# Two layers of attention and feed-forward on one core: the input of layer one's projections moves from the tile xf into four rows of the gelu tile g, and the order is picked anew

## The chip, the cores and the metric

The kernel runs on one core of a Trainium2 chip. The time is that of one execution on the device, in microseconds (us). Before the change it is 1430.3 us, the median of three runs (1429.61 to 1430.81).

TensorE (PE) multiplies matrices and writes to PSUM, ScalarE (ACT) computes exponentials and gelus, VectorE (DVE) does copies, additions and layernorms, GpSimd (POOL) works on integers in SBUF, and SyncE (SP) issues the DMAs. PEld is the weight loading of TensorE.

## The reference

One sequence of 2048 tokens, width 512, in bf16, goes twice through the same two blocks, with the same weights. The attention has 32 heads of 16.

```python
def _A_ref(x, wqkv, wo):
    qkv = (x @ wqkv).reshape(B, S, 3, H, Dh) ...
    scores = jnp.einsum("bhqd,bhkd->bhqk", q, k) * (Dh ** -0.5)
    p = _softmax(scores, axis=-1)
    o = jnp.einsum("bhqk,bhkd->bhqd", p, v)
    return (o back to B, S, D) @ wo
def _B_ref(x, w1, b1, w2, b2):            # F = 1792
    h = _gelu(jnp.einsum("bsd,df->bsf", x, w1) + b1)
    return jnp.einsum("bsf,fd->bsd", h, w2) + b2
x = A_x
x = x + _A_ref(_layernorm(x), A_wqkv, A_wo)
x = x + _B_ref(_layernorm(x), B_w1, B_b1, B_w2, B_b2)
x = x + _A_ref(_layernorm(x), A_wqkv, A_wo)
x = x + _B_ref(_layernorm(x), B_w1, B_b1, B_w2, B_b2)
```

## The kernel before

**Cells.** The 2048 queries are cut into four segments of 512 (the last one of layer one into two of 256). A score cell is one matmul (L1432): 128 keys by 512 columns of queries, for one group of heads. There are 4096 cells in both layers. ScalarE computes the exponential of most cells, two or three at a time, from PSUM into units of 512 columns called "pt" (`exps`, L1879). VectorE takes other cells: it writes one scaled integer form of the scores (L1601, into the tiles "du"), POOL makes three more from it by integer additions (L1691, L1695), and the four are multiplied with scaled copies of V. The product with V (`pvs`, L1945) takes one matmul for a cell of ScalarE and four for one of VectorE. Four such matmuls stand side by side in TensorE.

**Units.** There are 20 pt units of their own. More are lent by tiles that are idle for a while: Q once a segment's attention is done, parts of K and V, and the 14 rows of the gelu tile `G` (128 x 14 x 512). `lent_g` gives the rows of `G` to the exponentials when a segment's feed-forward is done ("gfree"), and takes all of them back once the next segment's layernorm has landed, before its feed-forward may begin ("g1"). A search takes the first free units in a fixed sequence of blocks: first the own ones, then the lent ones.

**Around the attention.** While the attention of a segment runs, the post-processing of the segment before runs beside it (`post`): the output projection (`wo`, added to x at L1046), a layernorm (`ln`; its last step on VectorE is L802, the normalisation is L828) which a DMA transpose (L834) writes into the tile `XF`, seven pairs of up-projections (`hpair`, matmuls of L647, bias added by VectorE into `G` at L1155), the gelu in two halves (L1176), and four down-projections (`ytile`, added to x at L1207). In layer zero a second layernorm follows, with the same transposes, and twelve projections of layer one for that segment's 512 tokens (`projections`, `proj`): four K, four V, four Q, copied out of PSUM at L912 and L930. All of these matmuls are issued through L647.

**What xf holds.** In layer zero `XF` holds first the input of the feed-forward and then, after the second layernorm, the input of the projections of layer one. So in `post` the next segment's layernorm has two gates: "xfree" (all pairs of the previous feed-forward have read `XF`) and, when the previous segment was in layer zero, "pfree" (all twelve projections have read it):

```python
gate = [("xfree",) + prev] if prev else []
if prev and prev[0] == 0:
    gate.append(("pfree",) + prev)
```

**Order.** The order of each engine's instructions is fixed when the kernel is built. Each piece of work is a thread with a rank (a low number goes first): 10 for `wo`, 12 for the pairs and the gelu, 13 for the down-projections, 15 for the projections of layer one. `when` lets parts begin after a set share of the following attention has been scored. A model of the engines' clocks (`_Sched.run`) takes at each step the instruction that could start first. Twelve constants of that model (`KNOBS`) are set anew after each 24 us (`STRETCH`) of ScalarE's time, from one of 16 rows (`ORDERS`), chosen by the 60 entries of `PICKS`. A gate is therefore a matter of this order: an instruction whose token comes later is placed later in its engine's queue, and the engine does other work in the meantime. In the chip's program semaphores protect each tile.

**Queues.** SP issues weight loads and transposes in one queue. The weights go through a ring of five buffers of 256 KB ("wr", L1098), and a load waits until its buffer is free.

Of the kernel before, what the change touches and what calls it, by code (L numbers as in the profile page):

```python
# [18 lines left out]
NDC = D // 128  # L19
# [5 lines left out]
THIRD = (2, 5)  # L25
PT_RING = 20
WSEG = 2
LEND = (1, 0)
QP_RING = 3
W_RING = 5  # L30
# [80 lines left out]
)  # L111
STRETCH = 24
PICKS = (1, 13, 1, 1, 13, 13, 1, 2, 1, 13, 1, 13, 13, 1, 1, 14, 1, 13, 13, 13, 13, 11, 3, 1,
         1, 13, 13, 13, 13, 13, 13, 1, 13, 13, 13, 1, 13, 1, 1, 1, 1, 3, 13, 13, 5, 1, 13, 13,
         1, 0, 1, 1, 13, 13, 13, 13, 1, 1, 1, 13)
LOG2E = 1.4426950408889634
E_SCALE = 0.25 * LOG2E * 128
E_BIAS = 15992.765054484162
# [145 lines left out]
class _Sched:  # L264
# [164 lines left out]
    def tune(self):  # L429
        k = min(int(self.clock["act"] // STRETCH), len(PICKS) - 1)  # L430
        if k != self.stretch:
            self.stretch = k
            globals().update(zip(KNOBS, ORDERS[PICKS[k]]))
            LATENCY["pe"] = PE
# [84 lines left out]
def bass_interleave_layers__mha_block__dense_activation_gelu__prompt_kernel(  # L519
# [15 lines left out]
    with ExitStack() as es:  # L535
# [18 lines left out]
        T["WR"] += [pt[:, PT_RING - 4 + 2 * i:PT_RING - 2 + 2 * i, :].rearrange("p c f -> p (c f)") for i in range(2)]  # L554
        T["PT"] = [pt[:, :, :]] + [T["K"][1][:, :, 512 * c:512 * c + 512] for c in LEND]
        T["PT"] += [T["Q"][:, :, 512 * c:512 * c + 512] for c in range(S // 512)]
# [80 lines left out]
class _Plan:  # L637
# [221 lines left out]
    def proj(self, l, kind, i, c, src, skeys, ph, done):  # L859
# [53 lines left out]
        if kind == "K":  # L913
            keys = ["K%d.%d.%d" % (l, i, c)]
            if l == 1:
                keys += ["XL.%d" % t for t in range(4 * c, 4 * c + 4)]
                if c in LEND:
                    yield ("need", ("k1", c))
                    keys += self.lentkeys(LEND.index(c))
                elif c >= 2:  # L920
# [3 lines left out]
        elif kind == "Q":  # L924
            if l:
                yield ("need", ("q1", 0, c))
            yield _Op(ev, DV, lambda e: copy(e, T["Q"][:, i, cols], pb), reads=["B.%d" % b] + first,
                      writes=["Q.%d.%d" % (i, c)] + (self.lentkeys(len(LEND) + c) if l else []))
        else:
# [7 lines left out]
    def projections(self, l, c, prio):  # L937
        T = self.T
        if l == 0:
            def src(dc, t):  # L940
                return T["K"][1][:, dc, t * 128:(t + 1) * 128] if t is not None else T["K"][1][:, dc, 512 * c:512 * c + 512]
            skeys = ["XL.%d" % t for t in range(4 * c, 4 * c + 4)]
        else:
            def src(dc, t):
                return T["XF"][:, dc, (t % 4) * 128:(t % 4) * 128 + 128] if t is not None else T["XF"][:, dc, :]
            skeys = ["XF.%d" % j for j in range(4)]
        ph = self.phase[c]
        units = []
        if l == 1:
            units = [("K", b) for b in range(4)] + [("V", 4 * c + b) for b in range(4)] + [("Q", b) for b in range(4)]  # L950
        else:
            for b in range(4):
                units.append(("K", b))
                if c == 0:
                    units.append(("Q", b))
                units.append(("V", 4 * c + b))
            if c > 0:
                units += [("Q", b) for b in range(4)]
        for j, (kind, i) in enumerate(units):
            p = prio + (0.01 * j if l else 0.5 if kind == "Q" and c > 0 else 0)  # L960
            if l:
                yield ("cond", self.when(0, (c, 0, 512), JB + JS * j))
            if l == 0 and kind == "Q" and c > 0:
                yield ("cond", lambda i=i: self.scored >= QAT[c] + QSTEP * i)
            yield ("spawn", self.proj(l, kind, i, c, src, skeys, ph, (kind, l, i, c)), p)
# [136 lines left out]
    def wmore(self):  # L1102
        self.wover = {}
        yield ("cond", lambda: self.scored >= self.base[(NL - 1, self.segs[-1][WSEG])])
        us = range(PT_RING - 4, PT_RING)
# [74 lines left out]
    def ytile(self, l, seg, t):  # L1180
# [30 lines left out]
        if l == NL - 1:  # L1211
            yield _Op("sp", 1.0, lambda e: e.dma_start(self.hbm["out"][:, t, :], T["X"][:, t % XT, :]), reads=["X.%d" % (t % XT)],
                      writes=["OUT.%d" % t], sem="dout", by=16, tail=2.0)
            yield ("give", ("xout", t))

    def when(self, l, seg, part):
        return lambda: self.scored >= min(self.base[(l, seg)] + part * self.span[(l, seg)], self.total)

# [5 lines left out]
    def post(self, l, seg):  # L1224

        T = self.T
        tiles = self.tiles(seg)
        c = seg[0]
        last = (l, seg) == (NL - 1, self.segs[l][-1])
        prev = self.before(l, seg)  # L1230
        hb, hs, yb, ys = PACE.get((l, c), (HB[l], HS[l], YB[l], YS[l]))
        yield ("need", ("otn", l, seg, 3))
        for t in tiles:
            yield ("spawn", self.wo(l, seg, t), 10)
        self.phase[c] = 2 * l + 1
        xf, xk = lambda t: T["XF"][:, :, (t % 4) * 128:(t % 4) * 128 + 128], lambda t: ["XF.%d" % (t % 4)]
        gate = [("xfree",) + prev] if prev else []
        if prev and prev[0] == 0:
            gate.append(("pfree",) + prev)
        for ts in ([t] for t in tiles) if last else (tiles,):  # L1240
            yield ("spawn", self.ln(ts, xf, xk, LNP, last, gate), 0.2 if last else LNP)
        for t in tiles:
            yield ("need", ("xready", t, 2 * l + 1))
        yield ("give", ("ofree", l, seg))
        for t in tiles:
            yield ("need", ("lnt", t, 2 * l + 1))
        yield ("need", ("g1", l, seg))
        for p in range(NFC // 2):
            yield ("cond", self.when(l, seg, hb + hs * p))
            yield ("spawn", self.hpair(l, seg, p), 12 + 0.1 * p)  # L1250
        if not last:
            yield ("spawn", self.gelu(l, seg), 12)
        if not last:
            for p in range(NFC // 2):
                yield ("need", ("h", l, seg, p))
            yield ("give", ("xfree", l, seg))
        for i, t in enumerate(tiles):
            yield ("cond", self.when(l, seg, yb + ys * i))
            yield ("spawn", self.ytile(l, seg, t), 13)
        if l < NL - 1:  # L1260
            self.phase[c] = 2 * l + 2
            xp, pk = lambda t: T["XF"][:, :, (t % 4) * 128:(t % 4) * 128 + 128], lambda t: ["XF.%d" % (t % 4)]
            for ts in (tiles[:2], tiles[2:]):
                yield ("spawn", self.ln(ts, xp, pk, LNP), LNP)
        for t in tiles:
            yield ("need", ("xready", t, 2 * l + 2))
        yield ("give", ("gfree", l, seg))
        if l == NL - 1:
            return
        for t in tiles:  # L1270
            yield ("need", ("lnt", t, 2 * l + 2))
        yield from self.projections(l + 1, c, 15)
        for kind in "KVQ":
            for i in range(4):
                yield ("need", (kind, l + 1, 4 * c + i if kind == "V" else i, c))
        yield ("give", ("pfree", l, seg))
# [457 lines left out]
    def setup_units(self):  # L1734
        self.blocks, self.alias, self.closed = [(0, PT_RING)], {}, set()
        for c in LEND:
            lo = self.blocks[-1][1]
# [28 lines left out]
    def lent_g(self):  # L1766
        lo, hi = self.blocks[self.gblock]
        for c in range(self.NQ):
            for kind in "KVQ":
                for i in range(4):  # L1770
                    yield ("need", (kind, 0, 4 * c + i if kind == "V" else i, c))
        for l in range(NL):
            for seg in self.segs[l]:
                prev = self.before(l, seg)
                if prev:
                    yield ("need", ("gfree",) + prev)
                if seg[1] == 0:
                    self.closed.difference_update(range(lo, hi))
                    for u in range(lo, hi):
                        yield ("rel", "pt", u)  # L1780
                    for t in self.tiles(seg):
                        yield ("need", (GBACK[0], t, 2 * l + GBACK[1]))
                    self.closed.update(range(lo, hi))
                    for u in range(lo, hi):
                        yield ("take", ("pt", u))
                yield ("give", ("g1", l, seg))

# [6 lines left out]
    def lend_units(self):  # L1794
        for i, c in enumerate(LEND):
            self.s.spawn(self.lent(c, *self.blocks[1 + i]), 4)
# [261 lines left out]
```

## Time and profile before

| | us |
|---|---|
| median of three runs | 1430.3 |
| the profiled execution | 1429.75 |
| its span, first to last instruction | 1427.9 |
| ScalarE busy | 1401.1 |
| TensorE matmuls busy | 1385.5 |
| VectorE busy | 1216.6 |
| POOL busy | 997.9 |
| last L1018 of layer zero's segments, start | 196.2, 371.7, 542.9, 716.2 |
| last L1018 of layer one's first segment, start | 951.6 |

L1018 is the transpose of a finished piece of attention output. Four of them end a segment's attention, so these marks cut the span into stages: between two marks runs the attention of one segment with the post-processing of the one before. The last mark ends a longer stage, because layer one's first two segments begin on the keys that are ready and finish later.

A line of the groups in the profile reads: line, engine, operation, tile written <- tiles read, shape, count | busy us, mean ns of one | idle us of the engine before them, and what ended it. The granted clock of TensorE was 1.000 over the whole span.

### The profile page before, as it was taken

What the parts mean: (1) busy time and instruction counts of PE and PEld (TensorE: products, weight loads), DVE (VectorE), ACT (ScalarE), POOL (GpSimd) and SP (SyncE); (2) the same over time, 40 slices, a digit from 0 to 9 for tenths busy, and PEclk for the clock granted to TensorE, in tenths of its full rate; (3) what the DMA queues carried; (4) which work ended last, traced back from release to release, by engine and by line L of the source; (5) the groups of instructions that cost most, each with busy time, mean ns of one, the idle gap of its engine ahead of it and who ended that gap; (6) DMA issues with size and microseconds to landing.
All of it is one profiled execution on the core that took longest, in us unless ns stands there. A gap on an engine that the chain in (4) does not pass through costs nothing.

```text
span 1427.9 us, 45603 instructions
## 1 busy us (share of the span) xinstructions
PE 1385.5 (97%) x19402; PEld 420.7 (29%) x19402; DVE 1216.6 (85%) x2293; ACT 1401.1 (98%) x1406; POOL 997.9 (70%) x1256
## 2 busy tenths in 40 slices
PE   8999999999999999999999999999999999999999
PEld 3222222222222222222222222222222222344346
DVE  7789999788997889987998678899869977898684
ACT  7999999999999999999999999999999999999995
POOL 1086988668786787876767667757767977788661
PEclk9999999999999999999999999999999999999999
DMA  6100001261121611115411161101162105421522
GB/s 176 45 2 2 2 16 39 62 183 54 46 39 53 187 60 39 39 31 157 119 39 46 53 187 59 31 14 33 39 189 79 32 24 168 145 32 40 175 75 89
DMA packets 145187, 103.47 MB, mean 72 GB/s; under 512 B 37084, under 2 KB 143964, under 8 KB 144988
## 3 DMA queue, kind: packets, MB, share of 16 engines
q1 hardware_dynamic: 144988, 100.57, 25.2%
q8 instruction: 156, 2.56, 0.8%
q14 instruction: 43, 0.35, 0.1%
HBM read 88.74 MB, written 4.19 MB: 65 GB/s over the span
## 4 chain that ended last, share of the span: by engine, by line
ACT 67%; PE 24%; DVE 7%; POOL 2%; issue 1%; ACTq 0%; POOLq 0%
ACT pt L1879 50%; PE ps L1945 8%; PE ps L1432 8%; PE ps L647 7%; ACT q L1879 4%; ACT g L1879 3%; ACT g L1176 3%; ACT v L1879 3%; DVE du L1601 3%; ACT kt L1879 2%; POOL du L1695 1%; DVE kt L1601 1%; PE ps L1420 1%; ACT L1879 1%; ACT L1176 1%
## 5 line engine op out<-in xcount | busy, mean ns | idle before, releaser
L1879 ACT ACTIVATE pt<-ps 128x1024 bf16<-128x1024 f32 (+1 forms) x1085 | 1091.2, 1168 | 1.3 <-PE ps L1432 0.4
L1601 DVE TENSOR_SCALAR du<-ps 128x512 uint16<-128x512 f32 x894 | 597.2, 684 | 112.5 <-PE ps L1432 107.9
L1432 PE MATMUL ps<-qp,kt 32*128 32x512 bf16 x4096 | 537.4, 384 | 18.5 <-ACT pt L1879 11.2
L1695 POOL INT64_ADD du<-du x454 | 464.6, 1025 | 72.9 <-DVE qp L1380 9.6
L1691 POOL INT64_ADD du<-du x454 | 273.6, 605 | 231.9 <-DVE du L1601 180.8
L1945 PE MATMUL ps<-du,vc 128*17 128x512 bf16 (+1 forms) x2979 | 360.3, 360 | 2.3 <-POOL du L1695 0.6
L1432 PEld LDWEIGHTS ps<-qp,kt 32*128 32x128 bf16 x4096 | 143.2, 91 | 569.6 <-ACT pt L1879 177.9
L1945 PE MATMUL ps<-pt,v 128*17 128x512 bf16 (+1 forms) x2621 | 306.5, 359 | 4.3 <-ACT pt L1879 2.7
L1945 PE MATMUL ps<-du,v 128*17 128x512 bf16 (+1 forms) x993 | 166.3, 360 | 3.6 <-DVE v L988 1.0
L647 PE MATMUL ps<-xf,wr 128*32 128x512 bf16 (+1 forms) x2272 | 162.0, 371 | 0.4 <-DMA xf<-pt 0.2
L1601 DVE TENSOR_SCALAR kt<-ps 128x512 uint16<-128x512 f32 x202 | 136.2, 683 | 22.0 <-PE ps L1432 20.6
L1945 PE MATMUL ps<-kt,vc 128*17 128x512 bf16 (+1 forms) x732 | 145.1, 344 | 0.8 <-POOL du L1691 0.8
L1945 PEld LDWEIGHTS ps<-du,vc 128*17 128x17 bf16 x2979 | 95.6, 89 | 81.4 <-issue 35.6
L1695 POOL INT64_ADD kt<-kt x104 | 105.3, 1013 | 15.7 <-DVE ra L797 3.8
L647 PE MATMUL ps<-wr,g 128*32 128x512 bf16 x1504 | 110.7, 383 | 1.1 <-ACT g L1176 1.1
L1945 PEld LDWEIGHTS ps<-pt,v 128*17 128x17 bf16 x2621 | 74.2, 88 | 79.1 <-issue 53.2
L1945 PE MATMUL ps<-v,vc 128*17 128x512 bf16 (+1 forms) x405 | 90.4, 351 | 0.1
L1155 DVE TENSOR_SCALAR g<-ps,hb1t 128x512 bf16<-128x512 f32 (+1 forms) x112 | 79.0, 706 | 10.2 <-PE ps L647 9.8
L1601 DVE TENSOR_SCALAR v<-ps 128x512 uint16<-128x512 f32 x116 | 78.2, 682 | 11.0 <-PE ps L1432 10.6
L1691 POOL INT64_ADD kt<-kt x104 | 62.3, 599 | 35.6 <-DVE kt L1601 17.2
L1879 ACT ACTIVATE q<-ps 128x1024 bf16<-128x1024 f32 (+1 forms) x78 | 82.0, 1128 | 0.0
L1945 PE MATMUL ps<-kt,v 128*17 128x512 bf16 (+1 forms) x334 | 79.4, 354 | 1.9 <-POOL du L1695 0.9
(108 smaller groups left out, 1462.4 us busy)
## 6 DMA issues: line engine op xcount, KB each, us to landing
wr<-in_B_w_dram SPq DMA_DIRECT2D x243, 256.0 KB, 3.1
wr<-in_A_wqkv_dram SPq DMA_DIRECT2D x24, 256.0 KB, 2.8
wr<-in_A_wo_dram SPq DMA_DIRECT2D x17, 256.0 KB, 3.0
x<-in_A_x_dram SPq DMA_DIRECT2D x7, 512.0 KB, 4.9
pt<-in_B_w_dram SPq DMA_DIRECT2D x13, 256.0 KB, 3.9
kept<-x SPq DMA_DIRECT2D x4, 512.0 KB, 3.1
x<-kept SPq DMA_DIRECT2D x4, 512.0 KB, 3.9
out_dram<-x SPq DMA_DIRECT2D x16, 128.0 KB, 2.9
```

The lines of the kernel that those rows point to most:

```text
L647: return [lambda e, a=a: e.matmul(out[32 * a:32 * a + 32, :], lhsT=lhsT[:, 32 * a:32 * a + 32], rhs=rhs, start=start, stop=stop, tile_posi ...
L1155: yield _Op("dve", 0.21 + n / 966, lambda e, fc=fc, pb=pb: e.tensor_scalar(T["G"][:, fc, q], pb, T["HB1T"][:, fc:fc + 1], None, op0=ALU.ad ...
L1176: lambda e, g=g: e.activation(out=g, in_=g, func=ACT.Gelu_apprx_tanh), reads=gk, writes=gk, prio=2)
L1420: fns.append(lambda e, o=o, w=w, a=a, m=m: e.matmul(o, lhsT=w, rhs=rhs, start=start, stop=start, tile_position=(0, m * a)))
L1432: return (lambda e: e.matmul(o, lhsT=lhsT, rhs=rhs, start=True, stop=True, tile_position=(32 * a, 0)), ["K%d.%d.%d" % (l, gb, kt // 4), "Q ...
L1601: yield _Op("dve", 0.682, lambda e: e.tensor_scalar(u, self.bank(b), E_SCALE, E_BIAS, op0=ALU.mult, op1=ALU.add), reads=["B.%d" % b], writ ...
L1691: yield _Op("pool", 0.151 + 0.2176 * n, lambda e: e.int64_add(words(1, 1), words(0, 1), SHIFT * ONES), reads=key[0], writes=key[1])
L1695: yield _Op("pool", 0.143 + 0.4352 * n, lambda e: e.int64_add(words(2, 2), words(0, 2), 2 * SHIFT * ONES), reads=key[0] + key[1], writes=k ...
L1879: yield _Op("act", 0.052 + 0.4267 * n, lambda e, src=src, dst=dst: e.activation(out=dst, in_=src, func=ACT.Exp, scale=0.25), reads=["B.%d" ...
L1945: op.fns.append(lambda e, o=o, lhsT=q[0][0][m], rhs=q[0][1][:, n * m:n * m + n], a=a, st=st, sp=sp: e.matmul(o, lhsT=lhsT, rhs=rhs, start= ...
```

## The change

The second layernorm of layer zero writes its transposes into rows 10 to 13 of `G` instead of `XF`, and the projections of layer one read them there. These rows are dead once the down-projections of the same tokens have read them. The gate "pfree" on the next layernorm is gone. The rank of the projections goes from 15 to 11.5. For the segments whose predecessor is in layer zero, `lent_g` lends 10 rows instead of 14. In `PICKS` 19 of 60 entries differ: 3, 7, 10, 13 to 16, 21 to 24, 27, 28, 30, 31, 34, 37, 52 and 56, counted from zero.

```diff
+XP = 10
+PROJ = 11.5
...
-PICKS = (1, 13, 1, 1, 13, 13, 1, 2, 1, 13, 1, 13, 13, 1, 1, 14, 1, 13, 13, 13, 13, 11, 3, 1,
-         1, 13, 13, 13, 13, 13, 13, 1, 13, 13, 13, 1, 13, 1, 1, 1, 1, 3, 13, 13, 5, 1, 13, 13,
-         1, 0, 1, 1, 13, 13, 13, 13, 1, 1, 1, 13)
+PICKS = (1, 13, 1, 4, 13, 13, 1, 1, 1, 13, 13, 13, 13, 13, 12, 1, 13, 13, 13, 13, 13, 13, 13, 13,
+         13, 13, 13, 1, 1, 13, 1, 13, 13, 13, 1, 1, 13, 13, 1, 1, 1, 3, 13, 13, 5, 1, 13, 13,
+         1, 0, 1, 1, 1, 13, 13, 13, 14, 1, 1, 13)
...
             def src(dc, t):
-                return T["XF"][:, dc, (t % 4) * 128:(t % 4) * 128 + 128] if t is not None else T["XF"][:, dc, :]
-            skeys = ["XF.%d" % j for j in range(4)]
+                return T["G"][:, XP + dc, (t % 4) * 128:(t % 4) * 128 + 128] if t is not None else T["G"][:, XP + dc, :]
+            skeys = [k for j in range(4) for k in self.xpkeys(j)]
...
+    def xpkeys(self, t):
+        return ["G.%d.%d" % (f, t % 4) for f in range(XP, XP + NDC)]
...
         gate = [("xfree",) + prev] if prev else []
-        if prev and prev[0] == 0:
-            gate.append(("pfree",) + prev)
...
-            xp, pk = lambda t: T["XF"][:, :, (t % 4) * 128:(t % 4) * 128 + 128], lambda t: ["XF.%d" % (t % 4)]
+            xp, pk = lambda t: T["G"][:, XP:XP + NDC, (t % 4) * 128:(t % 4) * 128 + 128], self.xpkeys
...
-        yield from self.projections(l + 1, c, 15)
+        yield from self.projections(l + 1, c, PROJ)
...
                 if seg[1] == 0:
-                    self.closed.difference_update(range(lo, hi))
-                    for u in range(lo, hi):
+                    us = [u for u in range(lo, hi) if not (prev and prev[0] == 0 and XP <= u - lo < XP + NDC)]
+                    self.closed.difference_update(us)
+                    for u in us:
                         yield ("rel", "pt", u)
...
-                    self.closed.update(range(lo, hi))
-                    for u in range(lo, hi):
+                    self.closed.update(us)
+                    for u in us:
                         yield ("take", ("pt", u))
```

## The prediction

> **What bounds the kernel now.** I read the busy times first, then the idle times of ScalarE by its groups, then stage windows cut at the ends of the attention of each segment, then VectorE's timeline where the changed wait sits.
>
> ```profile
> span 1427.9 us, 45603 instructions
> ...
> PE 1385.5 (97%) x19402; PEld 420.7 (29%) x19402; DVE 1216.6 (85%) x2293; ACT 1401.1 (98%) x1406; POOL 997.9 (70%) x1256
> ...
> L1879 ACT ACTIVATE pt<-ps 128x1024 bf16<-128x1024 f32 (+1 forms) x1085 | 1091.2, 1168 | 1.3 <-PE ps L1432 0.4
> L1601 DVE TENSOR_SCALAR du<-ps 128x512 uint16<-128x512 f32 x894 | 597.2, 684 | 112.5 <-PE ps L1432 107.9
> ```
>
> ScalarE (ACT) is busy 98% of the span, and the idle time ahead of its largest group is 1.3 us in 1085 instructions. It takes the exponentials of most score cells (L1879). VectorE takes the others in a cheaper form that POOL completes (L1601): 894+202+116 = 1212 by the three L1601 groups of the page. All cells are 4096, one score matmul each (L1432 x4096), so ScalarE has 2884. A wide exponential of two cells costs 866.1 us / 905 = 0.957 us in the groups kept apart by shape, **0.48 us a cell**. With ScalarE always fed, a change pays only if VectorE, POOL and TensorE (PE) take more cells, at 0.48 us each. TensorE is the partner that runs out: 97% busy.
>
> The stages confirm it. The last transpose of a segment's attention output (L1018) starts at 196.2, 371.7, 542.9, 716.2 and 951.6 us, so the segments of layer zero after the first take 175.5, 171.2 and 173.3 us for 512 cells each. The busy times in windows between these marks (columns: window, length, then busy us of PE, PEld, DVE, ACT, POOL, the granted clock, DMA):
>
> ```profile
> 372.00:543.00 171.00, 168.23 (x2188) 46.15 (x2184) 150.24 (x281) 170.67 (x174) 127.97 (x158) 1.00 0.28 75
> 543.00:716.00 173.00, 169.46 (x2211) 46.00 (x2207) 153.57 (x288) 172.61 (x175) 128.84 (x160) 1.00 0.28 79
> 716.00:952.00 236.00, 227.48 (x2963) 62.85 (x2955) 197.72 (x370) 235.60 (x232) 161.00 (x206) 1.00 0.22 63
> ```
>
> ACT is full in each; PE is within 9 us of full. The first and the second window hold the same work per segment: a post-processing of the segment before, with its projections of layer one.
>
> **Part one: the wait that goes.** Before, the layernorm that writes tile xf for a segment waits, when its order is fixed at build time, for the token that the previous segment's twelve layer-one projections are done, since they read xf. VectorE's timeline shows where that ends last (start, length, instruction):
>
> ```profile
> 569.53 0.15 DVE L802 SCALAR_TENSOR_TENSOR nmr<-mv,rstd 128x4 f32<-128x4 f32 x1
> ...
> 579.11 0.68 DVE L912 CAST q<-ps 128x512 bf16<-128x512 f32 x1
> 579.71 0.68 DVE L1601 TENSOR_SCALAR du<-ps 128x512 uint16<-128x512 f32 x1
> 580.31 1.37 DVE L828 TENSOR_SCALAR pt<-x,rstd,nmr 128x512 bf16<-128x512 bf16 x4
> ```
>
> The statistics are complete at 569.7 (L802); the four normalisations (L828) follow only at 580.3, behind the last Q cast (L912). That is 10.6 us. In segment three L802 ends at 744.15, the last Q cast starts at 750.96 and L828 at 751.57: 7.4 us. In segment one the last Q cast starts at 373.3, long before L802 ends (395.3), and L828 comes at 395.8: no wait. In (1,0) L802 ends 972.1 and the last Q cast started at 915.3: no wait. So the gate binds **in two segments of four**. Nothing idles in it: VectorE's order simply holds other work there. What goes is therefore not idle time but crowding: LN, 14 feed-forward pairs' additions and the down-projection all come later, and meet the next attention's work.
>
> Its worth I take from the stage rows. The segment whose window holds a gated layernorm took 173.3 us, the one before without a gate 171.2: **2.1 us**. For the long stage after 716.2 (704 cells in 235.4 us, 2.99 a us; 512/171.2 is also 2.99) the same comparison gives nothing lost. So the bounds are 0 (the difference is order and not the gate) and 4.2 us (both segments). I take 4.2, since the gated pair is also where two queues back up: weight loads and transposes, below.
>
> After the gate the next to be late is the landing of the transposes and the return of the lent gelu tiles. The four transposes of xf issue at 580.74 to 584.6 and land by 588.1; the first feed-forward cast (L1155) is at 593.5. On SP's queue they are moved ahead of the weight load issued at 579.05. That load waits then for at most their 5.98 us, against 596.25 for the next load; it hides behind the seven paced pairs. The four normalisations of 1.37 us move ahead of two Q casts on VectorE; both are there anyway.
>
> **Part two: where the projection input goes.** 16 DMA transposes, 512 Q and K matmuls and 256 V matmuls change their tile from xf to g. Same engine, shape and count: 0 us. As weights the page has both: 383 ns with g (L647 ps<-wr,g) against 384 with xf (ps<-wr,xf). As the moving operand g stands in ps<-g,kt (382 ns, the V projections of layer zero, whose weights lie in g) against a median of 380 ns with xf: 512 x 2 ns, four side by side, are 0.3 us at most, and I take 0. The second layernorm now waits for the down-projection's reads of g, but it needs that projection's sum in x anyway (L1207): 0.
>
> New waits: the casts into g rows 10 to 13 of the next segment must follow the projections that read them. Those casts begin with the eleventh L1155 of a segment: 440.9, 630.5, 800.5 and 1018.6 us, against last Q casts at 373.3, 579.1, 751.0 and 915.3. The nearest has 49.5 us, and about 39 when the feed-forward comes 10.6 us earlier. Cover enough: 0. If it were gone, the cast on VectorE would hold the exponentials queued behind it, 0.69 us each. The projections' rank of 11.5 instead of 15 keeps them ahead of the next feed-forward (12), which the gate did before: 0.
>
> **Part three: four buffers fewer.** Between the segments the 14 gelu rows are lent to the exponentials; now 10 are, after each layer-zero segment. By the trace's exponentials into g (2 or 3 cells each) less the L1945 matmuls that read g, the lent rows are occupied up to 14 at 360 to 384 us, 10 at 528 to 576, 14 at 744 and 12 at 888. They are the overflow that lets TensorE put off the product with V. Four fewer are four products done earlier, 306.5 us / 2621 = 0.117 us each by the L1945 group of pt: 0.47 us of TensorE. The peak at 744 falls into the wait that goes, so two peaks remain, at 360 and 888: **0.9 us**. If TensorE isn't short just then it costs 0; the upper end is a rival below.
>
> On whether TensorE is short at all, the trace has 97% for matmuls and 29% for weight loads, and 177.9 us in which weight loads of L1432 waited for exponentials. The Trainium skill (Perfetto Trace Analysis, Identifying the Most-Contended Engine) says that the share of matmul time is a poor measure, and that the share of weight loads and the achieved flops should be read instead. By that rule TensorE has room, part three would cost 0, and the sum would be 1426.1; no row here decides it.
>
> **Part four: the order picked anew.** 19 of 60 picks differ, each ruling the order for 24 us of ScalarE's time. Full stretches without a gelu hold about 72 to 79 cells, say 75, so one cell more or less is 24/75 = 0.32 us. The trace shows no other order. Bounds: one cell in each changed stretch, always the same way, is 6.1 us either way; at random sqrt(19) x 0.32 = 1.4 us. I take 0.
>
> **Sum.** The profiled execution took 1429.75 us (span 1427.9 and 1.85 around it), 0.55 below the median of 1430.3. -4.2 + 0.9 = -3.3; from the median, **1427.0 us**.
>
> **Rivals.**
>
> *Nothing comes of it* (chance 0.26): the wait lies on no engine that bounds. For it: the window 560 to 580 has ACT busy 20.00 us of 20.00 and PE 19.93, and 730 to 751 has 21.00 of 21.00 on both, so there is no gap to close; the stage after 716 shows no loss; and the scatter 171 to 175 us holds an ungated 175.5. Against: the same three stages can't rule out 2 us. It gives the median plus 0 to 0.9, about 1430.5. The same holds if the order picked anew leaves L828 where it was, so that the change doesn't do what it says. The Trainium skill (Perfetto Trace Analysis, Optimization Strategy) advises to look for gaps on the most contended engine and to make what they wait for earlier. By that rule this change would yield nothing, and the trace agrees that ACT has no gap there.
>
> *Slower, through the buffers* (0.32): with 10 rows the units run out, products of ScalarE's cells with V must go first, those of VectorE's cells wait, and their own buffers stay full, so VectorE gets fewer cells. It decides from the point at which more than 10 rows would be occupied. Price: the peaks at 360 to 396, 744 to 756 and 888 to 900 are 60 us. VectorE's cells stand at 22 per 24 us in the window 360 to 384, and at 17 in 936 to 960 where they are scarce. Some 4 lost per 24 us over 60 us are 10 cells, 4.8 us: **1435**. Against it: ACT shows no wait for space at the full 14.
>
> ```profile
> 360.00:384.00 24.00, 14.92 (x22) 1.00 0.16 46
> ...
> 936.00:960.00 24.00, 11.01 (x17) 1.00 0.01 2
> ```
>
> These two rows are L1601 alone (busy us and count); the first is the stretch where the lent rows fill up.
>
> **How the numbers follow.** The forecast case, faster, has 0.42 and its own range 1421 to 1427.4: the sum less part four's 6.1, up to the edge of 0.2%. No effect has 0.26, slower 0.32. Differences under 0.2% (2.9 us) are about what a measurement of this kernel can't tell from no change. The range of 1421 to 1435 runs from the sum with the whole gain by order to the buffer rival's price; I leave about 0.05 below and 0.1 above.
>
> **What would show it.** Right: L828 of segment two within 2 us of its L802, near 570, and segment three's near 740 to 745; the first L1155 some 8 to 12 us earlier; the marks of L1018 closer together, by 2 us each for two segments; more than 1212 cells in L1601. Part three: lent g rows at 10, ACT idle still near nothing, and as many L1601 at 360 to 384 as before. Wrong: L1018 marks unchanged though L828 is earlier (nothing comes of it), or L1601 fewer in the three peaks (buffers), or a difference that begins before 300 us, where only the order has changed.

## The result

| | before | after |
|---|---|---|
| median, 14 runs each | 1430.05 us | 1432.88 us |
| ratio, 95% interval | | 1.0019 [1.0011, 1.0027] |
| profiled execution (span) | 1429.75 (1427.9) | 1433.56 (1431.8) |
| cells on VectorE | 1212 | 1208 |

The changed kernel is 2.8 us slower, which 14 runs of each tell from no change, though it is under the 0.2% that the prediction took for the limit. The page after, the lines that answer to those of before (line numbers are 2 to 4 higher: L1883 is the exponential, L1604 VectorE's cell):

```profile
span 1431.8 us, 45629 instructions
...
PE 1388.9 (97%) x19430; PEld 422.7 (30%) x19430; DVE 1212.2 (85%) x2289; ACT 1403.7 (98%) x1408; POOL 995.2 (70%) x1248
...
L1883 ACT ACTIVATE pt<-ps 128x1024 bf16<-128x1024 f32 (+1 forms) x1081 | 1084.5, 1165 | 2.9 <-PE ps L1435 2.1
L1604 DVE TENSOR_SCALAR du<-ps 128x512 uint16<-128x512 f32 x890 | 594.0, 685 | 105.6 <-PE ps L1435 100.8
```

The span is 3.9 us longer. ScalarE works 2.6 us more of it, of which VectorE's four cells fewer (890+201+117 = 1208) explain 4 x 0.48 = 1.9 us; the other 1.3 us are idle time of ScalarE (28.1 us in the whole span against 26.8). The marks of L1018 (now L1020) start at 197.7, 371.9, 541.7, 715.1 and 954.6 us. So the stages show where the time went:

| stage, between marks (us) | to the first | 1st to 2nd | 2nd to 3rd | 3rd to 4th | 4th to layer one's first | rest of the span |
|---|---|---|---|---|---|---|
| before | 196.2 | 175.5 | 171.2 | 173.3 | 235.4 | 476.3 |
| after | 197.7 | 174.3 | 169.8 | 173.4 | 239.5 | 477.2 |

The changed kernel loses 1.5 us before any changed code has run (only two picks differ there; the experiments e1 and e2 below, with the lists exchanged, have this mark at 195.5 and 197.5, so it goes with the list). It is 1.1 us ahead at the fourth mark, and loses 4.1 us in the long stage behind it. From layer one's first mark on the two agree within 0.9 us. The windows of the three later stages (as shown of before: length, then busy us of PE, PEld, DVE, ACT, POOL, clock, DMA) have ScalarE idle for at most 0.9 us in each, so what is longer there is its work:

```profile
372.00:542.00 170.00, 167.36 (x2192) 45.64 (x2180) 150.05 (x283) 169.18 (x172) 129.13 (x160) 1.00 0.28 77
542.00:715.00 173.00, 169.17 (x2206) 46.15 (x2202) 147.32 (x280) 172.83 (x174) 124.24 (x152) 1.00 0.28 78
715.00:955.00 240.00, 232.81 (x3026) 65.10 (x3023) 203.37 (x379) 239.14 (x236) 165.53 (x212) 1.00 0.23 63
```

What the prediction said of the layernorm behind the gate came about. VectorE after, at the same place in segment two (start, length, instruction):

```profile
569.32 0.15 DVE L804 SCALAR_TENSOR_TENSOR nmr<-mv,rstd 128x4 f32<-128x4 f32 x1
...
570.68 1.38 DVE L830 TENSOR_SCALAR g<-x,rstd,nmr 128x512 bf16<-128x512 bf16 x4
...
586.51 0.69 DVE L914 CAST q<-ps 128x512 bf16<-128x512 f32 x1
...
590.83 0.74 DVE L1157 TENSOR_SCALAR g<-ps,hb1t 128x512 bf16<-128x512 f32 x1
```

The normalisation (L830) now follows its statistics at once, 9.6 us earlier than before, and no longer waits for the last Q cast. But the first feed-forward cast (L1157) comes at 590.8 against 593.5: only 2.7 us of the 9.6 arrive. In segment three the normalisation moves from 751.6 to 736.3 and the first cast from 761.4 to 758.2, 3.2 us. The last Q cast itself comes later than before: 586.5 (L914) against 579.1 in segment two, 754.4 against 751.0 in segment three. TensorE shows the same. These are the instructions that touch g and xf, in windows that end just after the first pair (count: durations; first and last start). Before:

```profile
L1945 PE MATMUL ps<-g,v x22: 378/382/386, 558.9 to 590.1; 128*17 128x512 bf16 x22
...
L1155 DVE TENSOR_SCALAR g<-ps,hb1t x1: 742/742/742, 593.5 to 593.5; 128x512 bf16<-128x512 f32 x1
```

The first pair of before, in the timeline (start, length, instruction):

```profile
590.97 0.61 PE L647 MATMUL ps<-xf,wr 128*32 128x512 bf16 x8
```

After:

```profile
L649 PE MATMUL ps<-g,wr x64: 378/380/391, 570.8 to 586.1; 128*32 128x512 bf16 x64
...
L1949 PE MATMUL ps<-g,v x12: 379/382/387, 558.3 to 581.0; 128*17 128x512 bf16 x12
```

```profile
L649 PE MATMUL ps<-xf,wr x32: 378/384/391, 588.0 to 594.8; 128*32 128x512 bf16 x32
```

Before, the last lent row of g is read at 590.1 (ps<-g,v), and the first pair follows at 591.0: the return of the lent rows looks like the last wait. After, the rows are back at 581.0, but the Q projections (ps<-g,wr) run until 586.1, and the first pair (ps<-xf,wr) starts at 588.0. The projections now have the better rank, so they seem to have taken the place of the gate that had waited for them. How far the rank does this, e6 below tests.

### The profile page after: what moved, and what is told of

Its sections match the earlier page's. It is cut to its first block, busy times and chain, and to the rows that moved or that the text cites. A ratio compares the mean times of both kernels' runs of the same rounds, so it can differ in the third digit from the quotient of the medians.

```text
span 1431.8 us, 45629 instructions
## 1 busy us (share of the span) xinstructions
PE 1388.9 (97%) x19430; PEld 422.7 (30%) x19430; DVE 1212.2 (85%) x2289; ACT 1403.7 (98%) x1408; POOL 995.2 (70%) x1248
## 4 chain that ended last, share of the span: by engine, by line
ACT 59%; PE 31%; DVE 6%; DMA 1%; POOL 1%; issue 1%; SPq 0%; ACTq 0%; DVEq 0%
ACT pt L1883 45%; PE ps L1435 10%; PE ps L1949 10%; PE ps L649 10%; ACT q L1883 4%; ACT g L1178 3%; DVE du L1604 2%; ACT v L1883 2%; ACT kt L1883 2%; ACT g L1883 2%; DVE kt L1604 1%; ACT L1883 1%; ACT L1178 1%; POOL du L1698 1%; DMA b1c<-in_B_b_dram 1%
## 5 line engine op out<-in xcount | busy, mean ns | idle before, releaser
L1883 ACT ACTIVATE pt<-ps 128x1024 bf16<-128x1024 f32 (+1 forms) x1081 | 1084.5, 1165 | 2.9 <-PE ps L1435 2.1
L1604 DVE TENSOR_SCALAR du<-ps 128x512 uint16<-128x512 f32 x890 | 594.0, 685 | 105.6 <-PE ps L1435 100.8
L1949 PE MATMUL ps<-du,vc 128*17 128x512 bf16 (+1 forms) x2967 | 351.9, 360 | 4.1 <-POOL du L1698 1.8
L1949 PE MATMUL ps<-pt,v 128*17 128x512 bf16 (+1 forms) x2593 | 300.9, 360 | 5.1 <-ACT pt L1883 1.7
L1604 DVE TENSOR_SCALAR kt<-ps 128x512 uint16<-128x512 f32 x201 | 135.9, 684 | 26.9 <-PE ps L1435 25.6
L1949 PE MATMUL ps<-kt,vc 128*17 128x512 bf16 (+1 forms) x726 | 136.3, 345 | 0.0
L649 PE MATMUL ps<-wr,g 128*32 128x512 bf16 x1760 | 129.7, 383 | 1.9 <-ACT g L1178 1.7
L649 PE MATMUL ps<-xf,wr 128*32 128x512 bf16 (+1 forms) x1760 | 122.9, 368 | 0.8 <-DMA xf<-pt 0.6
L1604 DVE TENSOR_SCALAR v<-ps 128x512 uint16<-128x512 f32 x117 | 78.7, 683 | 20.2 <-PE ps L1435 19.9
L1157 DVE TENSOR_SCALAR g<-ps,hb1t 128x512 bf16<-128x512 f32 (+1 forms) x112 | 79.1, 707 | 12.3 <-PE ps L649 12.3
L1883 ACT ACTIVATE q<-ps 128x1024 bf16<-128x1024 f32 (+1 forms) x83 | 88.3, 1136 | 0.1
L1949 PE MATMUL ps<-v,vc 128*17 128x512 bf16 (+1 forms) x411 | 87.4, 350 | 0.1
```

What stands on the lines that cost most here:

```text
L649: return [lambda e, a=a: e.matmul(out[32 * a:32 * a + 32, :], lhsT=lhsT[:, 32 * a:32 * a + 32], rhs=rhs, start=start, stop=stop, tile_posi ...
L1157: yield _Op("dve", 0.21 + n / 966, lambda e, fc=fc, pb=pb: e.tensor_scalar(T["G"][:, fc, q], pb, T["HB1T"][:, fc:fc + 1], None, op0=ALU.ad ...
L1604: yield _Op("dve", 0.682, lambda e: e.tensor_scalar(u, self.bank(b), E_SCALE, E_BIAS, op0=ALU.mult, op1=ALU.add), reads=["B.%d" % b], writ ...
L1883: yield _Op("act", 0.052 + 0.4267 * n, lambda e, src=src, dst=dst: e.activation(out=dst, in_=src, func=ACT.Exp, scale=0.25), reads=["B.%d" ...
L1949: op.fns.append(lambda e, o=o, lhsT=q[0][0][m], rhs=q[0][1][:, n * m:n * m + n], a=a, st=st, sp=sp: e.matmul(o, lhsT=lhsT, rhs=rhs, start= ...
```

## The experiments

Theory O: the order decides. A list of picks fits the code for which it was searched, and the code's parts are worth little. Theory M: the code costs the 2.8 us, by the four rows or by moving the feed-forward. All times are set against runs of the kernel before, taken along with them on the same chip (medians 1429.46 to 1430.17 us). With four runs of an experiment an interval reaches about 0.0015, 2.1 us, to each side. Two such distances add up to some 3 us, so a smaller difference between two experiments isn't told from none; such ones are read for their size and for whether both lists agree. Differences between experiments are taken between their distances to before.

**Lists crossed.** e1: the new code with the old list. e2: the old code with the new list.

```diff
# e1, in the changed kernel           # e2, in the kernel before: the other way round
-PICKS = (1, 13, 1, 4, 13, 13, 1, 1, ...
+PICKS = (1, 13, 1, 1, 13, 13, 1, 2, ...
```

> The changed code with the old PICKS. Theory O (the order decides: each list of picks fits the code it was searched for, and the code's parts are worth about nothing): worse than both kernels, by 3 to 8 us over before, 1433 to 1438, with fewer than 1212 cells on VectorE. Theory M (the code itself costs 2.8 us, through four lent rows fewer or through the earlier layernorms): 1433, as the changed kernel, whatever the picks.

> The old code with the new PICKS. Theory O: worse than both kernels, by 3 to 8 us over before, 1433 to 1438, since this list was not searched for this code. Theory M: as before, 1430, since the code is that of before; if the new picks are simply worse picks, 1433 here and 1430 for the new code with the old picks.

Measured: e1 1438.70 us, +8.8, ratio 1.0064 [1.0049, 1.0079]; e2 1438.62 us, +8.7, 1.0060 [1.0045, 1.0075]. Both are a little beyond O's upper end and 5.7 us or more over either kernel, with 1205 and 1201 cells on VectorE. Neither list is good or bad by itself: each does better with the code for which it was searched.

A weakness of e2, and of e3 and e8 below, must be said here. With these three lists the order that the old code builds leaves out one wait. Near 900 us it places a product with V of layer one (of key tile 14, 15 and 14) ahead of the copy that writes this V. `pvs` asks for the V of the first waiting cell of each column only, and one piece of its work can take two cells of a column. The semaphores of this program keep the order that was built; they add no dependence that it lacks. So the product reads what the lent unit held before. With the wait the order would be another one from there on, and no run has its time. The kernel before and all runs of the new code (e6 apart, see there) have every V written first, so the conclusions are drawn below from these where they can be.

**One list for both.** e3 and e4: row 13 for all picks. e8 and e9: a list drawn by chance from rows 1 and 13.

```diff
-PICKS = (...)
+PICKS = (13,) * 60                     # e3 old code, e4 new code
+PICKS = (13, 1, 13, 1, 13, 13, 1, ...  # e8 old code, e9 new code: the same 60 draws
```

> The old code with row 13 for all 60 picks, so that no search has fitted the order to the code. Theory O: some us above before, 1431 to 1438. Theory M says nothing of this one alone; it is the base of the next run.

> The changed code with row 13 for all 60 picks, against the old code with the same. Theory O: the two differ by up to 4 us with either sign. Theory M: the changed code is 2.8 us slower, with L1604 counts 4 to 8 lower.

> The old code with a list of picks drawn by chance between rows 1 and 13. Theory O: 1433 to 1442, and the changed code with the same list differs by up to 5 us, either sign. Theory M: the changed code is 2.8 us slower than this.

> The changed code with the same random list as the old code's 1440.9. Theory O: within 5 us of it, either sign; the mean of the three differences new less old (own and crossed lists aside: row 13 gave -0.7) stays within 2 us of 0. Theory M: 1443.7 or more.

Measured: row 13, old code 1435.48 us (+5.5, 1.0039 [1.0024, 1.0054]), new code 1434.77 (+4.8, 1.0034 [1.0023, 1.0045]). Random list, old code 1440.91 (+11.1, 1.0082 [1.0067, 1.0097]), new code 1438.34 (+8.9, 1.0063 [1.0048, 1.0078]). With the same list the new code is 0.7 and 2.2 us *faster*. M wanted it 2.8 us slower in both, 3.5 and 5.0 us away, so these runs speak against M, as far as the old code's times with these lists can be used. Nor has VectorE fewer cells with the new code: 1210 in e4 against 1205 in e3, 1207 in e9 against 1200 in e8. What needs no run of the old code: the new code alone takes 1434.8, 1438.3 and 1438.7 us with three lists that weren't searched for it, and 1432.9 with its own.

**The parts of the code, at one list.** e5 (row 13) and e10 (random list) put the gate back into the new code: ten rows lent, the projection input in g, the layernorm late.

```diff
 gate = [("xfree",) + prev] if prev else []
+if prev and prev[0] == 0:
+    gate.append(("pfree",) + prev)
```

> The changed code with the gate pfree put back into post and row 13 for all picks: ten rows lent and the projection input in g, but the layernorm waits as before. Theory O (order decides, parts worth about nothing): within 2 us of the two row 13 runs at 1435.5 (old code) and 1434.8 (new code). Theory M (the code's parts cost): 2 to 4 us over the old code at row 13 if the ten rows cost, 1437 to 1439.

> The changed code with the gate back and the random list: four rows fewer, the gate as before. Theory O: within 3 us of both the old and the new code on this list. Theory M by buffers: 2 to 4 us over the old code's 1440.9.

Measured: e5 1435.59 us (+5.8, 1.0042 [1.0027, 1.0056]), e10 1440.78 (+11.3, 1.0080 [1.0063, 1.0097]). Old code to gate back (e3 to e5, e8 to e10) is the price of the four rows, with the new place and rank of the projections: +0.2 and +0.2 us, nothing that can be seen, though e3 and e8 leave out the wait named above. Gate back to new code (e5 to e4, e10 to e9) is what the gate's removal brings, free of that weakness: -0.9 and -2.4 us. VectorE in segment two, first e5, then e4:

```profile
567.13 0.16 DVE L802 SCALAR_TENSOR_TENSOR nmr<-mv,rstd 128x4 f32<-128x4 f32 x1
...
589.70 1.37 DVE L828 TENSOR_SCALAR g<-x,rstd,nmr 128x512 bf16<-128x512 bf16 x4
600.08 0.74 DVE L1155 TENSOR_SCALAR g<-ps,hb1t 128x512 bf16<-128x512 f32 x1
```

```profile
569.56 0.15 DVE L802 SCALAR_TENSOR_TENSOR nmr<-mv,rstd 128x4 f32<-128x4 f32 x1
570.91 0.72 DVE L828 TENSOR_SCALAR pt<-x,rstd,nmr 128x512 bf16<-128x512 bf16 x2
571.56 0.73 DVE L828 TENSOR_SCALAR g<-x,rstd,nmr 128x512 bf16<-128x512 bf16 x2
...
591.86 0.74 DVE L1155 TENSOR_SCALAR g<-ps,hb1t 128x512 bf16<-128x512 f32 x1
```

With the gate the statistics lie 22.6 us before the normalisation, without it 1.4. The feed-forward starts 8.2 us earlier, and the whole kernel gains 0.9 us. The other lists agree: the first feed-forward cast of segment two comes at 584.2 in e1 and 581.6 in e12 (below), 9.3 and 11.9 us earlier than in the kernel before, as much as the prediction hoped for; the times are 8.8 us more and 1.1 us less (the 1.1 not told from nothing). Here an earlier feed-forward is worth little.

**More rows taken away.** e7 (row 13) and e11 (random list) lend two rows instead of ten.

```diff
-us = [u for u in range(lo, hi) if not (prev and prev[0] == 0 and XP <= u - lo < XP + NDC)]
+us = [u for u in range(lo, hi) if not (prev and prev[0] == 0 and u - lo >= 2)]
```

> The changed code with two rows of g lent after a layer-zero segment instead of ten, row 13: three times the loss of buffers against the old code. Theory M by buffers: the cost grows with the rows taken, 4 rows 3 us, 12 rows 8 or more, so over 1442, and more than in the row 13 run with ten. Theory O: within the scatter of orders, 1431 to 1441.

> Two rows of g lent instead of ten, random list. Theory M by buffers: as at row 13, some 10 us over the new code on the same list. Theory O: the 10.6 us at row 13 were mostly order; here within 5 us of the new code, either sign.

Measured: e7 1445.33 us (+15.5, 1.0114 [1.0097, 1.0131]), e11 1438.20 (+8.7, 1.0061 [1.0046, 1.0076]). At row 13 the eight rows more cost 10.7 us against e4, just as M by buffers wanted and 4.3 us beyond O's range; at the random list they cost nothing, -0.1 against e9. (Two runs of e7 had a granted clock of 0.998; the two at 1.000 took 1444.3 and 1444.6 us, still 9.6 us or more over e4.) One run alone would have seemed to prove the buffers. The trace of e7 shows little waiting for space. ScalarE's exponentials into pt in e7, and into the rows of g between 300 and 960 us:

```profile
L1881 ACT ACTIVATE pt<-ps 128x1024 bf16<-128x1024 f32 (+1 forms) x1120 | 1121.7, 1162 | 3.1 <-PE ps L1947 1.4 <-PE ps L1433 1.1
```

```profile
L1881 ACT ACTIVATE g<-ps x3: 1018/1116/1232, 355.0 to 743.2; 128x1024 bf16<-128x1024 f32 x3
```

Three exponentials use g, where e4 has 41, and the idle time ahead of the pt group is 3.1 us in all, 1.4 us of it ended by a product with V (L1947), which gives units back. ScalarE found other units; e7 has 1198 cells on VectorE against 1210 in e4, 12 x 0.48 = 5.8 of the 10.7 us. Fewer cells is also what the buffer rival named, so whether e7 lost them by the rows or by the order isn't shown; e11 has 1202 against 1207 in e9 and the same time. What else makes up e7's loss stays open.

**The rank.** e6 puts the projections back to rank 15, at row 13. With this rank the last Q projection of segments one and two reads rows that the next feed-forward's casts have already replaced, since no gate holds these back; the instructions and sizes are the same.

```diff
-PROJ = 11.5
+PROJ = 15
```

> The changed code with the projections' rank back at 15 and row 13. Theory R (the rank of 11.5 has taken the place of the gate: the feed-forward waits for the two free PSUM banks that the projections take first): where projections and the next feed-forward meet, the first L1157 follows the landing of xf by under 8 us instead of some 12, and starts earlier; the time changes by under 3 us either way if earlier feed-forward is worth nothing. If an earlier feed-forward is worth the 2.1 us a segment of the prediction, 1431 or less.

Measured: 1437.72 us, +7.9, 1.0052 [1.0037, 1.0067], 3.1 over e4, just at what can be told. Three of the four runs had a granted clock of 0.998 or 0.999, though; the one at 1.000 took 1435.04 us, +5.2 against e4's +4.8. The first cast is 9.0 and 9.9 us behind the landing of xf in segments two and three, against 13.0 and 10.5 in e4. So R's "under 8" is missed, and the rank explains some 4 us in segment two and little in three. The rank in fact moves one projection: only the last Q cast goes behind the pairs (643.5 and 809.9 against 587.8 and 759.1 in e4), and the other eleven projections still go ahead of the first pair. That the projections hold up the pairs through their rank is so shown in part; what else does stays open. The feed-forward is somewhat earlier and the kernel is no faster.

**A better list for the new code.** e12: the changed code, a third list, from a longer search.

```diff
-PICKS = (1, 13, 1, 4, 13, 13, 1, 1, ...
+PICKS = (1, 1, 12, 13, 8, 1, 1, 13, 1, 13, 13, 1, 1, 1, 13, 12, 1, 11, 1, 4, 13, 1, 1, 13,
+         1, 13, 4, 1, 1, 2, 1, 1, 13, 1, 1, 1, 13, 1, 1, 1, 13, 13, 10, 1, 13, 15, 1, 13,
+         1, 13, 3, 5, 13, 13, 13, 1, 1, 13, 1, 13)
```

> The changed code with a third list of picks, searched for this code for longer from a random start. Theory O: the 2.8 us were the list and not the code, so a list as well fitted as that of before brings the changed code to 1428 to 1431, within 0.2% of before and 2 us or more under the changed kernel's 1432.9. Theory M: the code keeps its 2.8 us, 1432 to 1434 at best.

Measured over 11 runs: 1429.06 us against 1430.17, ratio 0.9993 [0.9984, 1.0002]. That is 3.8 us under the changed kernel with nothing but the list different, as O expected and beyond M's 1432, and not told apart from before. Whether a search as long would also bring the old code further down was not run. The page of e12, whose order gives VectorE 899+201+115 = 1215 cells:

```profile
span 1427.3 us, 45743 instructions
...
PE 1387.3 (97%) x19478; PEld 420.6 (29%) x19478; DVE 1213.5 (85%) x2296; ACT 1400.1 (98%) x1403; POOL 1001.9 (70%) x1252
```

The long stage, from the fourth mark to layer one's first, spreads in the same way:

| | before | after | e1 | e2 | e3 | e4 | e5 | e6 | e7 | e8 | e9 | e10 | e11 | e12 |
|---|---|---|---|---|---|---|---|---|---|---|---|---|---|---|
| code | old | new | new | old | old | new | gate back | rank 15 | two rows | old | new | gate back | two rows | new |
| long stage, us | 235.4 | 239.5 | 244.0 | 245.1 | 242.8 | 237.8 | 237.0 | 238.0 | 241.1 | 244.3 | 239.6 | 245.3 | 238.5 | 234.9 |

It runs from 234.9 to 245.3 us, and both codes reach its lower end with a list that fits. Theory O stands: the same changed code takes 1429.1, 1432.9, 1434.8, 1438.3 and 1438.7 us with five lists. That the code itself is worth nothing at all isn't shown; at the two lists fitted to neither code no comparison of old, new and gate back finds more than 2.4 us, and some 3 us is the least that can be told.

## Why the prediction was wrong, point by point

The sum of the prediction, term by term, against the experiments (row 13: e3, e5, e4; random list: e8, e10, e9):

| term, us | forecast | by row 13 | by the random list |
|---|---|---|---|
| part one, the gate goes | -4.2 | -0.9 | -2.4 |
| part two, the place of the projection input | 0 | in part three | in part three |
| part three, four rows fewer | +0.9 | +0.2 | +0.2 |
| part four, the order picked anew | 0 | +3.5 | +5.0 |
| sum | -3.3 | +2.8 | +2.8 |

Both measured columns must add up to 2.8, since each goes step by step from the one kernel to the other. Each term is known to some 3 us, and those of parts three and four use e3 or e8, which leave out a wait.

- **The bound: right in the main.** ScalarE is 98% busy in all runs. Its cells don't give the whole time, though. Its busy time runs from 1400.1 (e12) to 1410.2 us (e7), and its idle time, which the prediction's sum has no term for, from 26.8 (before) to 32.5 us (e6); e4 has only two cells on VectorE fewer than before and is 4.8 us slower.
- **The gate binds in segments two and three only: right for the list of before.** The normalisations moved as forecast, to 570.7 (570 was named) and to 736.3 (earlier than the 740 to 745 named). Which segments are held up is a matter of the list: with the random one the gate also binds in segment one (e8: statistics at 390.6, normalisation at 398.9).
- **What is late next: partly wrong.** The return of the lent rows was named as a wait, and the trace before fits that (590.1, then the first pair). The rank of 11.5 was costed at 0 because it "keeps them ahead of the next feed-forward (12), which the gate did before". Keeping them ahead still delays the feed-forward: the first cast came 2.7 and 3.2 us earlier, not 8 to 12. By e6 the rank accounts for some 4 us in segment two and little in three. That the Q casts themselves end 7.4 and 3.4 us later than before was not foreseen.
- **The worth of the gate, 4.2 us: too large.** At a common list it is 0.9 and 2.4 us, neither told from nothing. It was the upper bound of a comparison of two stages (173.3 against 171.2) that differ by order: in e3 the gated stage has 172.3 against 168.7, in e8 180.1 against 172.5, and in e4, without the gate, 175.9 against 170.8. The prediction saw that 0 was as possible and took the end that favoured its case.
- **The four rows, 0.9 us: too large, and harmless.** Four rows cost 0.2 us twice, as far as e3 and e8 can be used. After the change the lent rows, counted as the prediction counts them, fill to 10 at 348 to 384 us, as forecast, but only to 8 at 888. In the window 360 to 384 VectorE's cells are 21 against 22, in 888 to 900 12 against 13. For four rows the rival by buffers, 4.8 us, fell with e5 and e10; for twelve the two lists disagree (10.7 and -0.1 us).
- **The order, taken as 0 with a bound of 6.1 us: the step that failed.** The bound was a fair one, but the term wasn't 0. Against row 13 the old list is worth 5.5 us to the old code and the new list 2.0 us to the new code (4.8 to 2.8 over before), so picking the order anew cost 3.5 us; against the random list it is 11.1 and 6.1, so 5.0 us. The old list, it seems, had been fitted to its code better than the new one to its own. e12 shows without any run of the old code that the list is what matters: another list takes 3.8 us off the changed code. Of the signs named beforehand, "a difference that begins before 300 us, where only the order has changed" is there (1.5 us at the first mark), and "L1018 marks unchanged though L828 is earlier" holds for the third-to-fourth stage: 173.3 and 173.4.
- **"Nothing comes of it" is close for the code.** That was the first rival. The Trainium skill (Perfetto Trace Analysis, Optimization Strategy) says to find the gaps on the most contended engine. ScalarE had none where the gate was, and removing the gate brought 0.9 and 2.4 us, neither of them told from nothing. With that rule this case's runs agree as far as they can tell.

## What to carry to other kernels

Where the order of work is searched for each version, two versions differ by the fit of the search as well as by their code; cross the two, or run both at several common orders, before either is praised or blamed. A list that was not searched for a code can also build an order that lacks a dependence, so see first that every tile is written before it is read. A wait that moves work in a planned order need not cost its length: here 8 us of earlier feed-forward came with 1 us. One suspected cost, enlarged at one order, can look proven (10.7 us) and be gone at the next (-0.1 us).
